# A prologue in an order of its own, and three of eight weight pairs rounded inside the main loop

## The chip, the cores and the metric

The kernel runs on one core of a Trainium2 chip. The metric is the device time of one execution in microseconds (us). Each median is over the executions named beside it. One execution of each kernel was recorded by the profiler; start times and durations below come from those records.

The core has a matrix engine (TensorE, PE in the profile, with PEld for its weight loads), VectorE (DVE), ScalarE (ACT), GpSimd (POOL), and a sync engine (SP) that here only issues transfers. Transfers are issued from SP, ACT and POOL; the profile counts them all on the same 16 DMA engines (in the first 180 us of the kernel before, 34.9% of these engines' time for SP's queue, 17.4% for ACT's and 12.6% for POOL's).

## The reference

```python
X = np.fft.rfft(x, axis=1)              # x: 8 batches x 3008 tokens x 256 channels
Y = X * (filt_r + 1j * filt_i)          # filters: 1505 frequencies x 256
y = np.fft.irfft(Y, n=3008, axis=1)
h = y.reshape(24064, 256) @ w_in        # 256 -> 2048
out = (h / (1 + np.exp(-h))) @ w_out    # silu(h) @ w_out, 2048 -> 256
```

The weights arrive as 64-bit floats and the kernel rounds them to 32 bits itself.

## The kernel before

The Fourier transform of a batch is a chain of small matrix products. **Stage 1** reads `x` in eight pieces (`load_x`), forms sums and differences on VectorE (`sums`), multiplies (`pa`), evicts from PSUM (`t`) and stores to DRAM (`d1`). **Six groups** then load that back (`t2`), run forward matmuls (`pb`), multiply by the filters on VectorE (`z`, `p`), add, run inverse matmuls (`pc`), evict (`q`) and store to DRAM (`d2`). **Stage 3** loads `t4`, multiplies (`pd`) and evicts to `y`. The main loop has 384 steps, bound by TensorE (busy for 49.86 of the first seven steps' 50.42 us), over all batches; the transforms of batch n+1 are spread over the steps of batch n. Only the first batch's transforms, and the rounding of the weights, lie ahead of the loop. The parts that matter, as they were:

```python
def load_filters():                       # 16 loads of 16 partitions each
    for j in range(4):
        s0, tau = slot_residue(0, 0, j), (1 if j % 2 == 0 else -1)
        for half in range(2):
            off, t = (s0, tau) if half == 0 else (94 - s0, -tau)
            for k, filt in enumerate((filt_r, filt_i)):
                p0 = 32 * j + 16 * half
                nc.scalar.dma_start(
                    out=f_t[k][p0:p0 + 16].rearrange("p g k c -> p (g k) c"),
                    in_=bass.AP(tensor=filt.tensor, offset=filt.offset + off * C,
                                ap=[[94 * C, 16], [t * C, 2 * NG], [1, C]]))

def evac(dst, src):                       # evictions alternate between two engines
    flip[0] ^= 1
    if flip[0]: nc.vector.tensor_copy(out=dst, in_=src)
    else:       nc.scalar.copy(out=dst, in_=src)

def add(g, k):                            # after the multiplication by the filters
    z, pt = prods[g][k]
    nc.vector.tensor_tensor(out=z[:, 0], in0=z[:, 0], in1=pt[:, 1], op=ALU.subtract)
    nc.vector.tensor_tensor(out=z[:, 1], in0=z[:, 1], in1=pt[:, 0], op=ALU.add)
# ... cut: stage 1, forward, multiply, inverse, stage 3, the main loop ...
def round_weights(j):                     # one of 16 weight matrices, 64 to 32 bits
    # ... cut: six instructions on VectorE, one on ScalarE, then on GpSimd:
    for w in range(2):
        gp.tensor_tensor(out=dst, in0=columns(mf[:, cols], w), in1=columns(ef[:, cols], w), op=ALU.mult)
    if j % 2:
        combine_weights(j // 2)           # four more on GpSimd for each pair
```

## Time and profile before

| | before |
|---|---|
| time, median of 3 (range) | 2809.41 us (2808.25 to 2809.86) |
| first forward matmul (`pb`) after stage 1 | 77.4 us |
| eviction of the last inverse (`q`, group 5) | 147.2 us |
| step 0 of the loop (its first copy `abc<-px`) | 180.25 us |
| steps 0 to 6, together | 50.42 us |
| first d1 store issued | 11.89 us |

The loop is TensorE's and is not touched after step 6, so the whole study is about the first 180 us, seven steps, and the last stores. The prediction shows the lines that say so.

### The profile page before, as it was taken

To read this page: it belongs to the slowest core of one execution; us is meant where nothing else is said; L and a number is where in the kernel's file an instruction comes from. 1 tells how busy PE (TensorE), PEld (TensorE's weight loads), DVE (VectorE), ACT (ScalarE), POOL (GpSimd) and SP (SyncE) were. 2 spreads that over 40 slices of the span, in tenths; PEclk is the share of its full clock that TensorE was granted. 3 is DMA by queue.
4 is the path that set the end of the run, shared out by engine and by line. 5 is a ranking of instruction groups with operands and counts; after the bars stand their busy time and mean duration, and the time that the engine had idled before them with its cause. 6 is when DMAs were issued, how large, how long until landed. Compare 5 with 4: busy or idle time off the path is not lost.

```text
span 2806.0 us, 39589 instructions
## 1 busy us (share of the span) xinstructions
PE 2671.0 (95%) x14592; PEld 2255.6 (80%) x14592; DVE 1671.9 (60%) x3528; ACT 1089.1 (39%) x2978; POOL 504.5 (18%) x739
## 2 busy tenths in 40 slices
PE   2469999999999999999999999999999999999997
PEld 0257889788897888878888888978888788898987
DVE  2866665666556665566655666566655666555554
ACT  0124334443344334443344433444344433444443
POOL 1531221112102120111111112012211211010100
PEclk9769999999999999999999999999999999999999
DMA  8543211232113211142103321133111422110000
GB/s 178 158 119 84 67 34 40 74 78 51 42 31 95 68 39 45 43 108 60 41 21 81 83 54 36 42 80 76 46 45 27 106 60 48 32 26 20 9 15 15
DMA packets 184546, 166.56 MB, mean 59 GB/s; under 512 B 121120, under 2 KB 151456, under 8 KB 184096
## 3 DMA queue, kind: packets, MB, share of 16 engines
q1 hardware_dynamic: 164624, 108.15, 16.0%
q0 software_dynamic: 17408, 50.35, 7.1%
q10 hardware_dynamic: 2320, 5.54, 1.1%
q8 instruction: 114, 1.87, 0.3%
q14 instruction: 80, 0.66, 0.1%
HBM read 88.97 MB, written 74.97 MB: 58 GB/s over the span
## 4 chain that ended last, share of the span: by engine, by line
PE 92%; DVE 4%; DMA 2%; issue 1%; POOL 0%; ACT 0%; SPq 0%; DVEq 0%; ACTq 0%; POOLq 0%
PE acc L467 40%; PE px L411 24%; PE pyz L411 17%; PE pd L341 4%; PE pc L319 3%; PE pa L267 2%; PE pb L290 2%; DVE g L382 1%; DMA x<-in_x_dram 1%; DVE u L255 1%; DVE z L310 0%; DMA d<-t 0%; DVE z L309 0%; DMA t<-d 0%; DMA filt<-in_filt_i_dram 0%
## 5 line engine op out<-in xcount | busy, mean ns | idle before, releaser
L467 PE MATMUL acc<-g,w_t 128*128 128x256 f32 (+1 forms) x5376 | 1512.6, 375 | 0.4 <-DVE g L382 0.4
L467 PEld LDWEIGHTS acc<-g,w_t 128*128 128x128 f32 x5376 | 1022.5, 190 | 114.4 <-DVE g L382 0.8
L382 DVE TENSOR_TENSOR g<-pyz,abc 128x256 f32<-128x256 f32 (+1 forms) x1152 | 479.7, 416 | 614.8 <-ACT abc L432 356.8
L382 DVE TENSOR_TENSOR g<-g 128x256 f32<-128x256 f32 (+3 forms) x1152 | 611.0, 530 | 196.6 <-ACT g L415 183.5
L411 PE MATMUL px<-ty,w_t 128*128 128x256 f32 (+1 forms) x2304 | 694.3, 383 | 0.5 <-ACT abc L432 0.5
L415 ACT ACTIVATE g<-g 128x256 f32<-128x256 f32 (+1 forms) x1152 | 473.0, 411 | 238.4 <-DVE g L382 235.9
L411 PEld LDWEIGHTS px<-ty,w_t 128*128 128x128 f32 x2304 | 419.5, 190 | 126.3 <-issue 72.1
L411 PE MATMUL pyz<-y,w_t 128*128 128x256 f32 (+1 forms) x1536 | 454.0, 377 | 8.5 <-DVE g L382 8.5
L382 POOL TENSOR_TENSOR s<-s 128x256 f32<-128x256 f32 (+1 forms) x329 | 265.7, 825 | 1040.4 <-DVE s L485 520.1
L411 PEld LDWEIGHTS pyz<-y,w_t 128*128 128x128 f32 x1536 | 282.9, 189 | 53.0 <-DVE g L382 15.8
L426 ACT COPY abc<-px 128x256 f32<-128x256 f32 (+1 forms) x384 | 141.4, 368 | 381.0 <-PE px L411 381.0
L415 ACT ACTIVATE g<-px 128x256 f32<-128x256 f32 (+1 forms) x384 | 145.8, 380 | 300.7 <-PE px L411 300.7
L432 ACT COPY abc<-px 128x256 f32<-128x256 f32 (+1 forms) x384 | 142.7, 372 | 285.0 <-PE px L411 284.8
L326 POOL DMA_DIRECT2D d<-q x192 | 113.9, 600 | 736.4 <-DVE q L209 736.3
L411 PE MATMUL pyz<-ty,w_t 128*128 128x256 f32 (+1 forms) x768 | 226.4, 377 | 0.0
L411 PE MATMUL px<-y,w_t 128*128 128x256 f32 (+1 forms) x768 | 225.7, 376 | 0.0
L411 PEld LDWEIGHTS pyz<-ty,w_t 128*128 128x128 f32 x768 | 145.7, 190 | 18.1 <-DVE g L382 2.0
L411 PEld LDWEIGHTS px<-y,w_t 128*128 128x128 f32 x768 | 144.7, 190 | 18.1 <-issue 0.4
L341 PEld LDWEIGHTS pd<-wi_t,t 96*128 96x128 f32 x1024 | 130.6, 201 | 21.4 <-issue 11.8
L341 PE MATMUL pd<-wi_t,t 96*128 96x94 f32 x1024 | 129.8, 283 | 17.6 <-issue 11.1
L319 PE MATMUL pc<-z,e_t 64*128 64x256 f32 x768 | 108.7, 422 | 37.3 <-DVE z L309 36.2
L419 ACT COPY abc<-px 128x256 f32<-128x256 f32 (+1 forms) x384 | 134.1, 349 | 0.1
(43 smaller groups left out, 1262.6 us busy)
## 6 DMA issues: line engine op xcount, KB each, us to landing
d<-t POOLq DMA_DIRECT2D x128, 192.0 KB, 3.0
t<-d SPq DMA_DIRECT2D x96, 256.0 KB, 4.1
d<-q POOLq DMA_DIRECT2D x192, 128.0 KB, 2.7
t<-d SPq DMA_DIRECT2D x64, 384.0 KB, 4.3
out_dram<-o SPq DMA_DIRECT2D x640, 32.0 KB, 1.8
x<-in_x_dram SPq DMA_DIRECT2D x128, 128.0 KB, 3.0
x<-in_x_dram SPq DMA_DIRECT2D x128, 60.0 KB, 2.9
raw<-in_moe_w_in_dram SPq DMA_DIRECT2D x16, 256.0 KB, 3.2
```

Source lines behind the costliest of these rows:

```text
L267: nc.tensor.matmul(out=ps[h][64 * par:64 * par + 64], lhsT=wf_t[rows, par], rhs=ut[rows, par], start=True, stop=True)
L290: nc.tensor.matmul(out=ps[k][32 * j:32 * j + 32, ri, :], lhsT=d_t[rows, 4 * g + at, ri, :], rhs=t2[rows, at, :], start=True, stop=True)
L319: nc.tensor.matmul(out=ps[i][:, k, :], lhsT=e_t[rows, g, k, ri, :], rhs=zs[k][rows, ri, :], start=(ri == 0), stop=(ri == 1))
L326: nc.gpsimd.dma_start(out=d2[a0:a0 + 2, :, :].rearrange("s n c -> n s c"), in_=qt[64 * p:64 * p + 64, :, :])
L341: nc.tensor.matmul(out=psv[:, i, :], lhsT=t4s[g][:, i, cb * 128:cb * 128 + 128], rhs=wi_t, start=True, stop=True)
L382: eng.tensor_tensor(out=out, in0=in0, in1=in1, op=op)
L411: nc.tensor.matmul(out=out, lhsT=w_t[:, c, 0, jp], rhs=rhs, start=start, stop=True, skip_group_check=True)
L415: nc.scalar.activation(out=g[:, k, 0:n], in_=g[:, k, 0:n] if src is None else src, func=AFT.Silu)
L419: nc.scalar.copy(out=sums[:, 0, 0:n], in_=xo)
L426: nc.scalar.copy(out=sums[:, 1, 0:n], in_=xo)
L432: nc.scalar.copy(out=sums[:, 2, 0:n], in_=xo)
L467: nc.tensor.matmul(out=acc[pair][i][:, h, 0:n], lhsT=w_t[:, c, 1, jp], rhs=g[:, k, 0:n], start=(jp == 0 and h == 0), stop=last, skip_group ...
```

## The change

Its intent: emit the first batch's transforms in a hand-made order instead of by the loop's plan. The loads come in the order of their use; `x` goes on two queues (sync and ScalarE); the filters move from ScalarE's queue to sync; the first batch's d2 stores move from GpSimd's queue to ScalarE's, and its adds from VectorE to GpSimd. One step of the rounding goes to ScalarE. Ten matrices are rounded ahead of the loop and six in steps 0 to 5. The last output stores use two queues.

```diff
 def load_filters():
-                    nc.scalar.dma_start(
+                    nc.sync.dma_start(
 def load_x(u):
+            if b == 0:
+                queue = (nc.sync, nc.scalar)[u % 2]
 def add(g, k):
-            nc.vector.tensor_tensor(...)        # both
+            eng = nc.vector if b > 0 else nc.gpsimd
+            eng.tensor_tensor(...)
 def inverse(g):
-                    nc.gpsimd.dma_start(out=d2[...], in_=qt[...])
+                    queue = nc.gpsimd if b > 0 else nc.scalar
+                    queue.dma_start(out=d2[...], in_=qt[...])
 def output(pair, chunk):
+                queue = nc.scalar if pair == len(pairs) - 1 and q % 2 else nc.sync
 def round_weights(j):
-        v.tensor_scalar(out=e, in0=e, scalar1=896.0, scalar2=0.0, op0=ALU.subtract, op1=ALU.max)
+        nc.scalar.activation(out=ef, in_=e, func=AFT.Relu, bias=bias_t)
# ... cut: buffers of their own for x, sums, raw and work ...
+    for u in range(8):
+        part["load_x"](u)
+    nc.sync.dma_start(out=d_t, in_=d_dram.ap())
+    weights(0)
+    load_filters()
# ... cut: sums and stage1 of the eight pieces, t2 loads, e table, weights 1 and 2, rounded 0 and 1 ...
+    for g in range(NG):
+        part["forward"](g)
+        for k in range(2):
+            part["multiply"](g, k)
+        for k in range(2):
+            part["add"](g, k)
+        if g > 0:
+            part["inverse"](g - 1)
+        if g % 2 == 0:
+            weights(3 + g // 2)
+        rounded(2 + g)
+    part["inverse"](NG - 1)
# ... cut: t4, rounded 8 and 9, stage 3 ...
+    for k in range(6):
+        put(k, 1, rounded, 10 + k)               # into steps 0 to 5
```

More of the change, by code (lines that the diff above doesn't have):

```diff
@@ L189 @@
     warm = cpool.tile([128, 1], FP32)
+    bias_t = cpool.tile([128, 1], FP32)
     x_t = [xpool.tile([128, 2, 2, C], FP32, name=f"x{i}") for i in range(2)]
@@ L234, in load_x @@
         def load_x(u):
-            if b == 0 and u < 4:
-                if u % 2 == 0:
-                    xs[u, "y"] = ypool.tile([128, 2, HALF], FP32, name=f"x_{b}_{u}", tag="y")
-                xs[u] = xs[u - u % 2, "y"][:, u % 2, 0:1024].rearrange("p (a n) -> p a n", a=2)
-                nc.gpsimd.memset(xs[u][32:64], 0.0)
+            queue = nc.sync
+            if b == 0:
+                queue = (nc.sync, nc.scalar)[u % 2]
+                if u in (0, 2):
+                    xs["y"] = ypool.tile([128, 2, HALF], FP32, name=f"x_{b}_{u}", tag="y")
+                if u < 4:
+                    xs[u] = xs["y"][:, u % 2, 0:1024].rearrange("p (a n) -> p a n", a=2)
+                elif u < 6:
+                    xs[u] = t4pool.tile([128, 2, 2 * C], FP32, name=f"x_{b}_{u}", tag="t4")
+                else:
+                    xs[u] = x_t[u % 2]
+                (nc.vector, nc.gpsimd)[u % 2].memset(xs[u][32:64], 0.0)
             else:
@@ L244, in load_x @@
                 for r0, nr in ((0, 32), (32, N1 - 32)):
-                    nc.sync.dma_start(
+                    queue.dma_start(
                         out=xs[u][64 * h + r0:64 * h + r0 + nr],
@@ L251, in sums @@
         def sums(u):
-            ut = upool.tile([128, 2, 512], FP32, name=f"u_{b}_{u}", tag="u")
+            if b > 0 or u % 3 == 0:
+                ut = upool.tile([128, 2, 512], FP32, name=f"u_{b}_{u}", tag="u")
+            else:
+                if u == 1:
+                    us["s"] = spool.tile([128, 2, 2, 512], FP32, name="u_s", tag="s")
+                ut = us["s"][:, u % 3 - 1]
             xt = xs.pop(u)
@@ L308, in add @@
             z, pt = prods[g][k]
-            nc.vector.tensor_tensor(out=z[:, 0], in0=z[:, 0], in1=pt[:, 1], op=ALU.subtract)
-            nc.vector.tensor_tensor(out=z[:, 1], in0=z[:, 1], in1=pt[:, 0], op=ALU.add)
+            eng = nc.vector if b > 0 else nc.gpsimd
+            eng.tensor_tensor(out=z[:, 0], in0=z[:, 0], in1=pt[:, 1], op=ALU.subtract)
+            eng.tensor_tensor(out=z[:, 1], in0=z[:, 1], in1=pt[:, 0], op=ALU.add)
         def inverse(g):
@@ L325, in inverse @@
                     a0 = p * NS + 2 * g + 12 * i
-                    nc.gpsimd.dma_start(out=d2[a0:a0 + 2, :, :].rearrange("s n c -> n s c"),
-                                        in_=qt[64 * p:64 * p + 64, :, :])
+                    queue = nc.gpsimd if b > 0 else nc.scalar
+                    queue.dma_start(out=d2[a0:a0 + 2, :, :].rearrange("s n c -> n s c"),
+                                    in_=qt[64 * p:64 * p + 64, :, :])
         def load_t4(g):
@@ L346, in stage3, with put, plan @@
                  psv)
+        return dict(load_x=load_x, sums=sums, stage1=stage1, load_t2=load_t2, forward=forward,
+                    multiply=multiply, add=add, inverse=inverse, load_t4=load_t4, stage3=stage3)
+    pending = []
+    def put(step, rnd, piece, *args):
+        pending.append((step + rnd / ROUNDS, len(pending), lambda: piece(*args)))
+    def plan(b, part):
         at = STEPS * b
-        pieces = []
-        def put(step, rnd, piece, *args):
-            pieces.append((at + step + rnd / ROUNDS, len(pieces), lambda: piece(*args)))
+        put(at - 49, 0, part["load_x"], 0)
+        put(at - 49, 0, part["load_x"], 1)
@@ L354, in spectral @@
         for u in range(8):
-            put(u - 48, 5, sums, u)
-            put(u - 47, 3, stage1, u)
-        put(-39, 0, load_t2, 0)
-        put(-39, 0, load_t2, 1)
+            put(at + u - 48, 5, part["sums"], u)
+            put(at + u - 47, 3, part["stage1"], u)
+        put(at - 39, 0, part["load_t2"], 0)
+        put(at - 39, 0, part["load_t2"], 1)
         for g in range(NG):
-            put(3 * g - (37 if b > 0 or g == 0 else 39), 3, forward, g)
-            put(3 * g - 37, 5, multiply, g, 0)
-            put(3 * g - 36, 1, multiply, g, 1)
-            put(3 * g - 36, 5, add, g, 0)
-            put(3 * g - 35, 1, add, g, 1)
-            put(3 * g - 35, 3, inverse, g)
@@ L367, in spectral @@
-        put(-18, 5, load_t4, 0)
-        for g, (step, rnd) in enumerate(((-16, 3), (-12, 3), (-8, 3), (-4, 3), (9, 3), (12, 6), (15, 6), (18, 6))):
-            put(step, rnd, stage3, 2 * g)
-            put(step, rnd, stage3, 2 * g + 1)
-        if b > 0:
-            put(-49, 0, load_x, 0)
-            put(-49, 0, load_x, 1)
-        return pieces, load_x
+            put(at + 3 * g - 37, 3, part["forward"], g)
+            put(at + 3 * g - 37, 5, part["multiply"], g, 0)
+            put(at + 3 * g - 36, 1, part["multiply"], g, 1)
@@ new lines, in plan, with plan_rest @@
+            put(at + 3 * g - 36, 5, part["add"], g, 0)
+            put(at + 3 * g - 35, 1, part["add"], g, 1)
+            put(at + 3 * g - 35, 3, part["inverse"], g)
+        put(at - 18, 5, part["load_t4"], 0)
+        for g, step in enumerate((-16, -12, -8, -4)):
+            for cb in range(2):
+                put(at + step, 3, part["stage3"], 2 * g + cb)
+        plan_rest(b, part)
+    def plan_rest(b, part):
+        for g, (step, rnd) in enumerate(((9, 3), (12, 6), (15, 6), (18, 6))):
+            for cb in range(2):
+                put(STEPS * b + step, rnd, part["stage3"], 8 + 2 * g + cb)
@@ L503, in output @@
                 p0 = 32 * q + 16 * rr
-                nc.sync.dma_start(
+                queue = nc.scalar if pair == len(pairs) - 1 and q % 2 else nc.sync
+                queue.dma_start(
                     out=bass.AP(tensor=out.tensor, offset=out.offset + t0 * C + 64 * q,
@@ L526, in columns, with load_weights @@
         return ap.rearrange("p (q k i) -> p k q i", q=4, k=2)
-    def load_weights(j):
-        raw = gpool.tile([128, 4, 512], U32, name=f"raw_{j}", tag="g")
-        nc.sync.dma_start(
-            out=raw[:, 0].rearrange("p (a n) -> p a n", a=2),
-            in_=moe_w_in.bitcast(U32)[:, 256 * j:256 * j + 256].rearrange("(a p) n -> p a n", p=128))
-        nc.sync.dma_start(out=raw[:, 1], in_=moe_w_out.bitcast(U32)[128 * j:128 * j + 128, :])
-        raws[j] = raw
+    def load_weights(jp):
+        if jp in (2, 5, 6, 7):
+            raw = spool.tile([128, 2, 2, 512], U32, name=f"raw_{jp}", tag="s")
+        else:
+            raw = gpool.tile([128, 2, 2, 512], U32, name=f"raw_{jp}", tag="g")
+        for i in range(2):
+            j = 2 * jp + i
+            nc.sync.dma_start(
+                out=raw[:, i, 0].rearrange("p (a n) -> p a n", a=2),
+                in_=moe_w_in.bitcast(U32)[:, 256 * j:256 * j + 256].rearrange("(a p) n -> p a n", p=128))
+            nc.sync.dma_start(out=raw[:, i, 1], in_=moe_w_out.bitcast(U32)[128 * j:128 * j + 128, :])
+        raws[jp] = raw
     def round_weights(j):
-        raw = raws.pop(j)
-        words = raw[:, 0:2].rearrange("p w (n t) -> p (w n) t", t=2)
+        words = raws[j // 2][:, j % 2].rearrange("p w (n t) -> p (w n) t", t=2)
         lo, hi = words[:, :, 0], words[:, :, 1]
-        e, m = raw[:, 2], raw[:, 3]
+        work = typool.tile([128, 2, 512], U32, name=f"work_{j}", tag="ty")
+        e, m = work[:, 0], work[:, 1]
         ef, mf = e.bitcast(FP32), m.bitcast(FP32)
@@ L547, in round_weights @@
                         op0=ALU.logical_shift_right, op1=ALU.bitwise_and)
-        v.tensor_scalar(out=e, in0=e, scalar1=896.0, scalar2=0.0, op0=ALU.subtract, op1=ALU.max)
-        v.tensor_scalar(out=e, in0=e, scalar1=255.0, scalar2=float(1 << 23),
+        nc.scalar.activation(out=ef, in_=e, func=AFT.Relu, bias=bias_t)
+        v.scalar_tensor_tensor(out=mf, in0=lo, scalar=2.0 ** -52, in1=mf, op0=ALU.mult, op1=ALU.add)
+        v.tensor_scalar(out=e, in0=ef, scalar1=255.0, scalar2=float(1 << 23),
                         op0=ALU.min, op1=ALU.mult)
@@ L552, in round_weights @@
                                op0=ALU.bitwise_and, op1=ALU.bitwise_or)
-        v.scalar_tensor_tensor(out=mf, in0=lo, scalar=2.0 ** -52, in1=mf, op0=ALU.mult, op1=ALU.add)
         for w in range(2):
@@ L559, in round_weights @@
         if j % 2:
+            raws.pop(j // 2)
             combine_weights(j // 2)
-        if j + 2 < NJ:
-            load_weights(j + 2)
     def load_exact(j):
@@ L579, in combine_weights @@
         combine(gp, w(S4), w(A12), w(S2), ALU.subtract)
-    def constants():
-        nc.scalar.dma_start(out=d_t, in_=d_dram.ap())
-        load_filters()
-        nc.scalar.dma_start(out=e_t, in_=e_dram.ap())
-        nc.scalar.dma_start(out=wi_t, in_=wi_dram.ap())
-    nc.sync.dma_start(out=wf_t, in_=wf_dram.ap())
-    for xt in x_t:
-        nc.gpsimd.memset(xt[32:64], 0.0)
-    pending = []
-    for b in range(B):
-        pieces, load_x = spectral(b)
-        pending += pieces
-        if b == 0:
-            for u in range(6):
-                load_x(u)
-            pending += [(-42.5 + k, 0, lambda k=k, load_x=load_x: load_x(6 + k)) for k in range(2)]
-            pending.append((-45, 0, constants))
@@ L600, with weights, rounded @@
-    if wide:
-        pending += [(-41.5, j, lambda j=j: load_weights(j)) for j in range(2)]
-        pending += [(-39 + 1.9 * j, NJ, lambda j=j: round_weights(j)) for j in range(NJ)]
-    else:
-        pending += [(-39 + 1.9 * j, NJ, lambda j=j: load_exact(j)) for j in range(NJ)]
+    def weights(jp):
+        if wide:
+            load_weights(jp)
+    def rounded(j):
+        if wide:
+            round_weights(j)
+        else:
+            load_exact(j)
+    nc.sync.dma_start(out=wf_t, in_=wf_dram.ap())
@@ new lines @@
+    nc.gpsimd.memset(bias_t, -896.0)
+    part = spectral(0)
+    for u in range(8):
[3 more added lines that the diff above has]
+    load_filters()
+    for u in range(3):
+        part["sums"](u)
+    for u in range(8):
+        part["stage1"](u)
+        if u + 3 < 8:
+            part["sums"](u + 3)
+    part["load_t2"](0)
+    part["load_t2"](1)
+    nc.sync.dma_start(out=e_t, in_=e_dram.ap())
+    weights(1)
+    weights(2)
+    nc.sync.dma_start(out=wi_t, in_=wi_dram.ap())
@@ new lines @@
+    rounded(0)
+    rounded(1)
+    for g in range(NG):
[10 more added lines that the diff above has]
+    part["inverse"](NG - 1)
+    part["load_t4"](0)
+    rounded(8)
+    rounded(9)
+    for u in range(8):
+        part["stage3"](u)
+    early[0] = None
@@ L605 @@
+    plan_rest(0, part)
+    for b in range(1, B):
+        plan(b, spectral(b))
+    for k in range(6):
+        put(k, 1, rounded, 10 + k)
+        if k in (1, 3):
+            put(k, 1, weights, 6 + k // 2)
     per = len(PAIRS) * 2
@@ L622 @@
     until(-1e-3)
-    early[0] = None
     for step in range(n_steps + LAG):
```

## The prediction

> **What bounds the kernel now.** I read three views: the page's slices, to see where TensorE is not busy; busy time by stage, to see what limits each part of that stretch; then waits and timeline inside it. The slices come first (PE busy tenths, 70 us a slice):
>
> ```profile
> PE   2469999999999999999999999999999999999997
> ```
>
> From the fourth slice on TensorE is full, so the time there is matmul time, which the change leaves alone. The first weight matmul of the main loop (L411) starts at 179.1 us; before it lie the first batch's transforms and the rounding of all weights. I cut these 179.1 us where the first forward matmul after stage 1 starts (77.4) and where the last inverse matmul ends (147.2). Columns: stretch, length, then busy time of PE, PEld, DVE, ACT, POOL, then clock, share of the 16 DMA engines, GB/s.
>
> ```profile
> 0.00:77.40 77.40, 21.52 (x66) 4.86 (x67) 21.95 (x37) 7.33 (x12) 17.45 (x31) 1.00 0.81 178
> 77.40:147.20 69.80, 32.29 (x286) 17.29 (x286) 60.42 (x108) 8.60 (x14) 41.16 (x58) 0.70 0.54 147
> 147.20:179.10 31.90, 14.34 (x65) 13.91 (x65) 23.41 (x35) 5.93 (x9) 20.90 (x26) 0.50 0.51 149
> ```
>
> Stage A is bound by transfers (engines of the DMA 81% busy, no compute engine over 28%); stage B by VectorE (60.4 of 69.8 us); stage C by a latency chain: store, load, matmul at half clock. The waits from 20 to 60 us say what A waits for (total us, times, longest):
>
> ```profile
> DVE t L209 <- DMA d<-t: 31.8, 2, 27.3
> ACT t L211 <- DMA filt<-in_filt_i_dram: 27.1, 1, 27.1
> ```
>
> The filter loads stand ahead of ScalarE's evictions in its own instruction stream and ahead of the d1 stores in the transfer engines. For B, the timeline shows what VectorE pays beside GpSimd (start, us, engine, line; the adds L309 and L310 are 128x256, 0.42 us when GpSimd is quiet):
>
> ```profile
> 93.71 0.65 DVE L309 TENSOR_TENSOR z<-z,p 128x256 f32<-128x256 f32 x1
> 94.16 3.39 POOL L382 TENSOR_TENSOR w_t<-w_t 128x256 f32<-128x256 f32 x4
> 94.29 0.94 DVE L310 TENSOR_TENSOR z<-z,p 128x256 f32<-128x256 f32 x1
> ```
>
> [...] the same add takes 0.42 us alone and 0.94 beside GpSimd. [...] the share was 0.95 from 20 to 40 us with three queues in use. [...] 0.73 us (2.90 for four) when undisturbed and 0.84 on average, against 0.42.
>
> **The change, part by part.** Stage A. The order by engine shows x going on two queues, then on the sync queue the d table, the first weight pair, the filters, the t2 loads, and only then the e table. Transfer work before the first forward matmul: over the first 180 us the sync queue took 34.9% of 16 engines for 16.99 MB (62.8 us, 3.7 us per MB), the GpSimd queue 12.6% for 6.29 MB (3.6 us per MB), the ACT queue 17.4% for 5.54 MB (31.3 us). The two tables are 2.36 MB of the last, 8.7 us at 3.7, so the filters (3.15 MB, runs of 1 KB in half of them) cost 22.6 us. Then x 3.08 MB = 11.4; d1 stores 3.15 MB = 11.3; d table 0.79 MB = 2.9; first weight pair 1.05 MB = 3.9; filters 22.6; first t2 half a MB = 1.9. Sum 54 us, plus 2 us until the first transfer and some 5 us of gaps (a tenth; a guess from the shares of 0.95 at best): 61 us for what starts at 77.4 now. Gone from in front of it are the e table (5.8 us) and the idle 19% . Gain 16.
>
> Stage B. VectorE loses 24 adds, and rounding falls from 16 matrices of six VectorE instructions to ten of five, eight of them before the last inverse is evicted. Per group g it then has four multiplies (0.60 us pitch, 2.4), one eviction (0.6) and one rounding. The rounding's own pitch is 0.33+0.46+0.61+0.46+0.61 = 2.5 us, but two of its instructions now wait for two ScalarE activations (0.63 each), and the order on ScalarE puts two d2 stores, an eviction (0.58) and two more stores ahead of these: 4 x 0.45 (the issue time of a filter load there) + 0.58 + 2 x 0.63 = 3.6 us after VectorE's eviction, and then 1.1 us for the last two instructions: 4.8 us for the rounding. So a group takes 2.4 + 0.6 + 4.8 = 7.8 us. GpSimd needs per group four adds, two products and on average two combinations, 8 x 0.85 = 6.8 us: just under, and off the path. The first two groups are slower by some 6 us in all, since e table and two weight pairs (3.7 MB, about 14 us) come only after t2: group 1's multiplies stand behind a rounding that waits for the second pair. From the first forward to the last inverse's eviction: 2 + 5 x 7.8 + 6 + the last group's 2.4 + 0.6 + 3.0 (its rounding is not delayed by much) = 53 us, against 69.9 (77.4 to 147.3). Gain 17.
>
> Stage C. Now the t4 loads stand behind weight loads that wait for roundings; the first is issued at 154.0, the third at 166.75. Afterwards two t4 loads go out as soon as the stores land: eviction and stores 5.5 us, load 4.3, then four groups of two at 3.6 us (7.11 us for four, half clock as now) plus about a microsecond for the third load: 25 us against 31.8. Gain 7. In sum the loop starts at 61 + 53 + 25 = 139 us, 40 earlier.
>
> What is moved into the loop. Six roundings fall into steps 0 to 5. A step there now looks so:
>
> ```profile
> 200.90:208.20 7.30, 7.30 (x38) 5.47 (x37) 4.57 (x10) 3.00 (x8) 1.00 (x2) 1.00 0.39 107
> ```
>
> VectorE has 4.57 us of work in 7.30; a rounding adds 2.6 us, GpSimd gets 1.5 us of products and every second step 3 us of combinations[...]. It fits by sum, but not by order: ScalarE's two activations stand ahead of the px copy that TensorE's next accumulation needs, and about 2 us late that copy eats most of the 1.1 us that the stage-1 matmuls give. I take 1 us a step, 6 us in all (an estimate, 2 to 12).
>
> The end. The last sixteen stores are issued one after another:
>
> ```profile
> 2796.01 7.51 SPq L504 DMA_DIRECT2D out_dram<-o  x16
> ```
>
> On two queues the issue takes half: 3.5 us off.
>
> Sum: 2809.4 - 40 + 6 - 3.5 = 2772 us.
>
> **The rivals.** First, stage 1 stays starved: the sync queue may have up to eight transfers outstanding, which in the filter phase are 1.5 MB or 11 us of slow traffic, and the d1 stores, two tiles deep, wait behind them as now (12 us from issue to landing at 44 us). For it: exactly this wait is in the trace. Against: the sum of transfers is the same in whatever order they are served, and once the filters are in, the last d1 stores find the engines free. It would make A 68 to 72: total 2780 to 2785. Second, GpSimd becomes the bound of B: it is at 6.8 us of a group's 7.8[...]; with roundings in between its instructions measured up to 0.98 us each (3.91 for four), then a group takes 9 us: 6 us more, 2778. Third, the ScalarE round trip is hidden because the sequencer issues stores faster than 0.45 us, and the groups run at VectorE's 5.5 us: 12 us less, 2760. Fourth, the loop's first steps hide the roundings wholly: 2766. Fifth, TensorE's clock, granted at half from 147 us on, comes back later than now: against it, it was full again 16 us after the loop's start, at 195 us, and the loop's start is unchanged.
>
> **Range and chances.** The three stage gains are uncertain by about 8, 8 and 4 us, the steps by 5; taken as independent some 13 us in all, so 2752 to 2792 should hold it 8 times in 10 (a little wider than 1.3 x 13, for what I have not seen). Faster by over 2% means under 2753.2: the prologue would have to shrink by some 59 us of 179, to 120, which needs the first and third doubts to fall well together: 0.12. Slower by over 2% needs a stall in the loop that goes on after step 5; nothing there is changed: 0.01.
>
> **What would show it.** In the changed profile: first forward matmul near 61 us, with the filter wait gone from ScalarE; q evictions about 7.8 us apart, each rounding's third VectorE instruction waiting on ScalarE; first L411-type matmul near 139; steps 0 to 5 about 8.3 us each and 7.26 after; a final store issue of about 4 us. If the forward matmul starts before 52 or after 70, the transfer sum is wrong; if groups are not paced by ScalarE, the chain in B is; if steps 0 to 5 take over 9.5 us each, the cost in the loop is.

Measured in the kernel before: the 128x256 add on VectorE, the share of the DMA engines, and an instruction of that size with two inputs on GpSimd (2.90 us for four of them from 76.98 us on; 0.838 us each over all 32 combinations of the weights), which the "8 x 0.85" of stage B rests on. The first rival's "up to eight transfers outstanding" can be read in the trace of the changed kernel: the fourth filter load (23.98 us) is issued only when the d table, eight places ahead of it on the sync queue, has landed, the next four when the four weight loads have, and the last eight when the first eight filter loads have.

## More of the kernel before

One line is added here, for what comes later: the seven first steps of the kernel before in one stretch (stretch, length, then busy time and instructions of PE, PEld, DVE, ACT and POOL, then clock, DMA share, GB/s).

```profile
180.25:230.67 50.42, 49.86 (x233) 36.20 (x234) 32.35 (x65) 20.43 (x56) 6.11 (x12) 0.96 0.37 98
```

TensorE is busy for 49.86 of 50.42 us and VectorE for 32.35: the steps have room on VectorE.

## The result

| | before | after | predicted after |
|---|---|---|---|
| time, median of 4 (range) | 2808.83 (2806.55 to 2809.86) | 2780.32 (2779.0 to 2781.49) | 2772 (2752 to 2792) |
| first forward matmul | 77.4 | 65.2 | 61 |
| first multiply, group 0 | 79.45 | 68.31 | – |
| eviction of the last inverse | 147.2 | 122.2 | 114 |
| step 0 of the loop | 180.25 | 147.62 | 140 |
| steps 0 to 6, together | 50.42 | 58.28 | 56.4 |
| from step 7 to the end | 2575.3 | 2571.9 | 3.5 less |

The changed kernel takes 0.9899 of the time before (95% interval 0.9882 to 0.9917): 28.5 us less, which is within 2%. Ratios here are the mean time of one kernel's runs over that of the other's of the same rounds, so not quite the ratio of the medians. The three parts add up: 32.6 us from the start, minus 7.9 in the steps, plus 3.4 at the end make 28.1; the profiled spans differ by 28.2.

In the page of the changed kernel TensorE's row of slices (tenths busy, 40 slices) differs from before only at its ends:

```profile
PE   3599999999999999999999999999999999999998
```

The same three stages as in the prediction, with the same columns, cut at the changed kernel's own events:

```profile
0.00:65.20 65.20, 18.51 (x65) 4.80 (x66) 24.65 (x39) 8.67 (x14) 15.72 (x30) 1.00 0.91 182
65.20:122.20 57.00, 33.50 (x288) 18.00 (x288) 36.82 (x59) 10.39 (x17) 32.91 (x46) 0.88 0.76 213
122.20:146.50 24.30, 14.08 (x65) 13.90 (x65) 10.35 (x16) 5.54 (x8) 10.43 (x14) 0.52 0.43 109
```

Stage A is 12.2 us shorter, stage B 12.8, stage C 7.6. A is more clearly a stage of transfers than before (share 0.91, was 0.81), yet it moves data at much the same rate (182 GB/s, was 178). In B, VectorE has lost its full row: 36.82 us of 57.00, where it was 60.42 of 69.80. Something else paces B now.

What waits in stage A (us in total, times, longest):

```profile
ACT t L211 <- DMA d<-t: 35.6, 6, 12.8
DVE t L209 <- DMA d<-t: 31.9, 5, 11.4
...
ACT t L211 <- DMA x<-in_x_dram: 14.5, 1, 14.5
```

Evictions of stage 1 wait for earlier d1 stores to land (the eviction's buffer is one of two), as before; and one new wait of 14.5 us ahead of ScalarE's very first eviction. The experiment that puts `x` back on one queue shows what it is worth.

In stage B, one group on ScalarE (start, us, engine, line, operation, tiles; ACTq is ScalarE's sequencer issuing transfers):

```profile
98.61 1.24 ACTq L340 DMA_DIRECT2D d<-q  x2
99.97 0.58 ACT L211 COPY q<-pc 128x512 f32<-128x512 f32 x1 [5.57 <-DVE work L574]
100.58 1.24 ACTq L340 DMA_DIRECT2D d<-q  x2
101.93 0.63 ACT L575 ACTIVATE work<-work 128x512 f32<-128x512 uint32 x1 [1.37 <-issue]
```

and what VectorE does about it:

```profile
102.59 0.69 DVE L579 SCALAR_TENSOR_TENSOR work<-raw,work 128x512 f32<-128x512 uint32 x1 [2.30 <-ACT work L575]
```

Two stores, the eviction, two more stores, and only then the activation that the rounding on VectorE waits 2.30 us for: the chain that the prediction had named. A store takes 0.62 us to issue. The groups' first multiplies start at 68.31, 77.39, 86.16, 95.50, 104.27 and 113.46 us: 9.03 us apart, not 7.8. The first of these intervals (9.08) has another cause than the four after it (8.77 to 9.34): group 0 has no stores ahead of its rounding, and VectorE waits for the weights instead:

```profile
74.58 0.43 DVE L574 TENSOR_SCALAR work<-raw 128x512 uint32<-128x512 uint32 x1 [3.79 <-DMA raw<-in_moe_w_out_dram]
```

The seven first steps, to be held against the line of before shown above:

```profile
147.62:205.90 58.28, 51.66 (x233) 35.26 (x234) 51.75 (x95) 26.70 (x68) 27.17 (x36) 0.98 0.45 121
```

VectorE goes from 32.35 to 51.75 us busy, GpSimd from 6.11 to 27.17, and TensorE idles for 6.6 us. Steps 1 to 5 take 8.61 to 8.63 each, step 6 again 7.28.

The last stores, on two queues side by side:

```profile
2771.31 3.70 SPq L529 DMA_DIRECT2D out_dram<-o  x8
2771.32 3.92 ACTq L529 DMA_DIRECT2D out_dram<-o  x8
```

### The profile page after: what moved, and what is told of

The parts are those of the page before. It is cut to its first block, busy times and chain, and to the rows that moved or that the text cites. A ratio compares the mean times of both kernels' runs of the same rounds, so it can differ in the third digit from the quotient of the medians.

```text
span 2777.8 us, 39564 instructions
## 1 busy us (share of the span) xinstructions
PE 2670.7 (96%) x14592; PEld 2253.3 (81%) x14592; DVE 1657.2 (60%) x3492; ACT 1098.0 (40%) x2994; POOL 505.1 (18%) x738
## 4 chain that ended last, share of the span: by engine, by line
PE 91%; DVE 4%; DMA 3%; ACT 1%; issue 1%; POOL 0%; ACTq 0%; SPq 0%; DVEq 0%; POOLq 0%
PE acc L491 39%; PE px L435 24%; PE pyz L435 17%; PE pd L355 4%; PE pc L332 3%; PE pa L279 2%; PE pb L302 2%; DMA d<-t 1%; DVE g L406 1%; DVE u L267 1%; DMA t<-d 1%; DMA x<-in_x_dram 0%; DVE z L323 0%; DMA raw<-in_moe_w_out_dram 0%; DVE z L322 0%
## 5 line engine op out<-in xcount | busy, mean ns | idle before, releaser
L340 POOL DMA_DIRECT2D d<-q x168 | 99.3, 597 | 728.1 <-DVE q L209 720.3
L284 POOL DMA_DIRECT2D d<-t x128 | 65.5, 516 | 329.7 <-ACT abc L456 283.7
```

The lines of the kernel that those rows point to most:

```text
L284: nc.gpsimd.dma_start(out=d1[par].rearrange("s p n c -> (s p) n c")[:, 4 * u:4 * u + 4, :], in_=t1[64 * par:64 * par + 2 * NS].rearrange(" ...
L340: queue.dma_start(out=d2[a0:a0 + 2, :, :].rearrange("s n c -> n s c"), in_=qt[64 * p:64 * p + 64, :, :])
```

## The experiments

Twelve kernels ran, in three calls of four, each on another chip; each has its own runs of the kernel before, whose medians were 2809.79 (7 runs), 2808.48 (7) and 2809.18 (7). Each experiment has four timed runs, its median and range below. "The changed kernel" is 2780.32 throughout. One warning from the profiles: with stage A untouched, the first multiply of group 0 still fell anywhere from 61.7 to 69 us between executions. So a start time from a single profile is worth several us.

### Stage B: what paces the groups

**The rounding ahead of the previous group's inverse** (so that its activations stand ahead of the stores on ScalarE).

```diff
             part["add"](g, k)
+        rounded(2 + g)
         if g > 0:
             part["inverse"](g - 1)
         if g % 2 == 0:
             weights(3 + g // 2)
-        rounded(2 + g)
```

> Edit: in the group loop each rounding stands before the inverse of the previous group, so that ScalarE has its two activations before the four d2 stores (4 x 0.62 us) and the eviction. Theory S (groups of stage B are paced by ScalarE: the rounding's third VectorE instruction waits for an activation behind four store issues): the rounding takes about 3 us in place of 5.5, the group period falls from 9.0 to about 6.8 to 7.2 (then GpSimd, eight instructions), stage B some 10 us shorter, about 2770 us. Rival G (GpSimd's eight instructions[...] pace the groups): no change within 2 us, 2779 to 2781.

Measured: 2776.21 us (2775.51 to 2778.8), ratio 0.9883 [0.9868, 0.9897]; groups 7.9 us apart on average ((108.42 - 68.99) / 5), and about 7.2 from group 1 on. The order on ScalarE did pace them. But the gain is 4 us, not five times 1.8: only four intervals have stores ahead of the rounding. Group 0 waits for its weights in both kernels (5.15 us in this profile, 3.79 in the other) and lasts 10.4 us, and from the last group's first multiply to the last eviction it is 10.5 us where it was 8.8.

**The first batch's d2 stores on the sync queue.**

```diff
-                    queue = nc.gpsimd if b > 0 else nc.scalar
+                    queue = nc.gpsimd if b > 0 else nc.sync
```

> Edit: the first batch's d2 stores are issued by the sync queue in place of ScalarE. Theory S: 2.5 us of issue a group leave ScalarE, so the period falls from 9.0 to about 7 and the kernel is about 10 us faster, unless the sync queue's own order (stores wait for evictions ahead of t2 and weight loads) delays a load; then 5. Rival G: no change within 2 us.

Measured: 2773.83 us (2771.63 to 2776.04), ratio 0.9873 [0.9856, 0.9889]; groups 8.0 us apart, the last eviction at 115.44, the loop from 140.11. ScalarE in one group:

```profile
89.97 0.59 ACT L211 COPY q<-pc 128x512 f32<-128x512 f32 x1 [7.03 <-DMA d<-q]
90.46 0.63 ACT L575 ACTIVATE work<-work 128x512 f32<-128x512 uint32 x1
```

The activation follows the eviction at once, so the issue of stores was the cost. In its place there is a new wait: the eviction's own buffer is one of two and waits for a store to land (`DMA d<-q`).

**The adds back on VectorE.**

```diff
-            eng = nc.vector if b > 0 else nc.gpsimd
+            eng = nc.vector
```

> Edit: the first batch's complex adds back on VectorE. Theory S: VectorE gets four adds of 0.34 us pitch before the eviction that everything on ScalarE waits for, so each of six groups is about 1.4 us longer: 8 us slower, 2788. Rival G: GpSimd loses four of its eight instructions a group (3 us), the period falls to 7 or less: about 10 us faster, 2770.

Measured: 2790.6 us (2784.22 to 2791.28), ratio 0.9927 [0.9912, 0.9942]: 10 us worse, with groups 10.6 us apart. The stage of the groups in this kernel's profile:

```profile
61.20:121.00 59.80, 31.13 (x263) 18.08 (x254) 41.45 (x80) 8.97 (x15) 14.84 (x20) 0.79 0.66 185
```

GpSimd falls to 14.84 us of 59.80 and the groups get slower, so GpSimd does not bound them (the second rival of the prediction). This edit also gives VectorE more to do; but the rounding-first kernel leaves GpSimd's work as it was, and its groups came down to 7.2 us. Moving the adds was worth some 10 us. The profile is of the fastest of the four runs, with an early stage A (first multiply at 61.67), which is why its loop start, 149.89, looks less bad than the median.

**Both: rounding first, and stores on sync.** The edits are the first two together.

> Edit: d2 stores of the first batch on the sync queue and rounding before the inverse, together. Theory S: once ScalarE is out of the way the groups run at GpSimd's 6.8 us or VectorE's 6.0[...], some 7 us each, so little is won over the stores on sync alone (whose groups took 8.0): about 3 us, 2771. Rival: both waits were independent and the two gains (4 and 6.5 us) add up: 2769 to 2770.

Measured: 2775.57 us (2774.59 to 2777.72), ratio 0.9881 [0.9867, 0.9896]. The two gains do not add; it is no better than the stores alone. The last eviction came at 117.83, against 115.44.

**Both, but the last group in the changed kernel's order** (rounding first only for `g < NG - 1`).

```diff
+        if g < NG - 1:
+            rounded(2 + g)
         if g > 0:
             part["inverse"](g - 1)
         if g % 2 == 0:
             weights(3 + g // 2)
-        rounded(2 + g)
+        if g == NG - 1:
+            rounded(2 + g)
```

> Stores of the first batch's d2 on the sync queue, and the rounding ahead of the inverse for all groups but the last, where the order stays as changed. If the last group's rounding ahead of its inverse is what made the two together no better than the stores alone: last inverse's eviction 2 to 3 us sooner than with both (117.8), loop start at 138 to 140, time 2769 to 2772. If instead the group's period is by then set by VectorE, whatever the order: groups of 7.5 us as with the stores alone, time 2773 to 2776.

Measured: 2773.76 us (2772.93 to 2776.44), ratio 0.9874 [0.9859, 0.9889]: equal to the stores alone, so the first theory's 2769 to 2772 failed and the rival's range holds, though not its reason. Groups are 7.9 us apart and the last eviction falls at 116.38. VectorE's evictions of the last two groups show what stands there:

```profile
109.69 0.69 DVE L209 COPY q<-pc 128x512 f32<-128x512 f32 x1 [1.23 <-DMA d<-q]
...
116.38 0.69 DVE L209 COPY q<-pc 128x512 f32<-128x512 f32 x1 [2.46 <-DMA d<-q]
```

VectorE is not full; its evictions wait for earlier stores to land before they may reuse their buffer. This is in the trace of this kernel; a kernel with a third buffer was not tried.

### Stage A: what fills the first 65 us

**The reversed filter rows read forwards.** Half of the filter loads read rows backwards, so that each row of 1 KB is a run of its own; here all read forwards in runs of 12 KB. The result is WRONG on purpose.

```diff
                 off, t = (s0, tau) if half == 0 else (94 - s0, -tau)
+                if t < 0:
+                    off, t = off - 2 * NG + 1, 1
                 for k, filt in enumerate((filt_r, filt_i)):
```

> Wrong result on purpose: the four loads of each filter that run backwards (runs of 1 KB) read the same rows forwards (runs of 12 KB). Same bytes. Theory T (stage A is the sum of the transfers, of which the filters are by far the dearest per byte): the first multiply starts some 5 us earlier than the 66 to 69 us of most runs so far, and the kernel is about 5 us faster, 2775. Rival Q (stage A is the queueing of d1 stores behind whatever is outstanding; the filters' slowness is their 16 partitions, not their direction): within 2 us of 2780.

Measured: 2781.72 us (2781.3 to 2783.44), ratio 0.9902 [0.9885, 0.9918]. Nothing changes: the first 66 us move 178 GB/s at a share of 0.90, where the first 65.2 us of the changed kernel move 182 at 0.91. The prediction's reason for slow filters, runs of 1 KB, falls.

**The filters after the first two t2 loads.**

```diff
     weights(0)
-    load_filters()
     ...
     part["load_t2"](1)
+    load_filters()
```

> Edit: the filter loads are issued after the first two t2 loads, so that the d1 stores have only the d table and the first weight pair beside them. Theory T: stage 1 ends much earlier (its evictions no longer wait 12 us for a store), but the filters' 23 us then stand between t2 and the first multiply: the multiply starts where it did, 66 to 69 us, or up to 4 us later, as the engines idle a little during stage 1 and the e table and weights come as much later; 2780 to 2785. Rival Q: the waits were lost time, and the first multiply starts 5 us earlier: 2775.

Measured: 2784.85 us (2782.85 to 2785.89), ratio 0.9913 [0.9898, 0.9927]: 4.5 us worse, first multiply at 73.62. Stage 1 is no longer starved (first forward matmul at 44.65), and VectorE's first multiply waits for filters:

```profile
73.62 0.69 DVE L314 TENSOR_TENSOR z<-pb,filt 128x512 f32<-128x512 f32 x1 [29.86 <-DMA filt<-in_filt_r_dram]
```

Whoever is served first, the filters' time has to be paid. This order also shows that time nearly by itself: the first filter load is issued at 43.82 and the multiply starts at 73.62, 29.8 us later, with no stage-1 store left beside them. But t2 loads still land until 48.5 us, and from 64.2 us on the e table and weights are under way too. A stretch in the middle, in which the filters are nearly all that is being moved, counts 133 GB/s at a share of 1.07, at which 3.15 MB take some 24 us (an estimate). The prediction had 22.6 us for it.

```profile
46.00:64.00 18.00, 3.99 (x62) 1.49 (x56) 0.00 (x0) 0.00 (x0) 2.14 (x4) 1.00 1.07 133
```

**The same bytes of filters in loads of 128 partitions.** Two loads in place of sixteen, one in runs of 12 KB and one in runs of 1 KB. Its output is wrong, which doesn't matter for the time.

```diff
-        for j in range(4): ...                  # 16 loads, each to f_t[k][p0:p0 + 16]
+        for k, filt in enumerate((filt_r, filt_i)):
+            nc.sync.dma_start(
+                out=f_t[k].rearrange("p g k c -> p (g k) c"),
+                in_=bass.AP(tensor=filt.tensor, offset=filt.offset,
+                            ap=[[10 * C, 128], [(1 + k) * C, 2 * NG], [1, C]]))
```

> WRONG on purpose: the same 3.15 MB of filters come in 2 loads of 128 partitions each (half of it in runs of 12 KB, half in runs of 1 KB, as in the changed kernel) in place of 16 loads of 16 partitions each; their values are not the right ones, the times don't depend on that. Theory D (the filters are slow because each load goes to 16 partitions [...]): the queue gets through them in about 10 us instead of some 21, the first multiply starts at 56 to 61 us instead of 66 to 70, and the time falls by 7 to 11 us, to about 2770. Rival V (what costs is the volume of all loads, 5.9 MB with weights and x, whatever partitions they go to): first multiply unchanged at 66 to 70, time 2778 to 2783.

Measured: 2764.71 us (2762.17 to 2765.18), ratio 0.9838 [0.9824, 0.9853]: 15.6 us better than the changed kernel, more than the 7 to 11 expected. First multiply at 51.95, loop from 131.31. The stretch in which the filters move, first in the changed kernel, then in this one (the last two numbers are DMA share and GB/s):

```profile
21.00:45.00 24.00, 6.85 (x27) 1.80 (x24) 5.58 (x9) 1.75 (x3) 3.01 (x6) 1.00 1.06 215
```

```profile
21.00:33.00 12.00, 4.51 (x19) 1.19 (x16) 3.69 (x6) 1.17 (x2) 2.01 (x4) 1.00 1.02 393
```

The DMA engines look equally full in both (1.06 and 1.02), and move 215 GB/s in one and 393 in the other. A full share is no proof of a full rate. The edit was made for the number of partitions that a load reaches, 16 before and 128 here, and the runs agree with theory D in direction: 133 GB/s where the filters moved nearly alone, in loads of 16 partitions, is about a third of 393. Why loads to few partitions should be slow was not shown. This run changes the number of loads, from 16 to 2, and the order of rows in DRAM as well, so the share of each is not separated.

**x on one queue again.**

```diff
-                queue = (nc.sync, nc.scalar)[u % 2]
+                queue = nc.sync
```

> All x loads of the first batch on the sync queue again (the loads by use, the adds and all else as changed). Theory T (stage A is bound by the sum of all transfers, and the two queues only change who issues): first multiply at 66 to 71 us, time within 3 us of the changed kernel, 2778 to 2783. Rival Q (two queues bring x sooner, or give it a larger share beside the filters): first multiply 4 us or more later, time 2784 or more. Rival R (the issues of x on ScalarE hold up its first evictions, which now wait until 16.8 us): the first stores go 3 us or more sooner and the first multiply comes 2 to 5 us sooner.

Measured: 2773.02 us (2772.15 to 2773.88), ratio 0.987 [0.9855, 0.9885]: 7.3 us better than the changed kernel, with no overlap between the four runs of each. Undoing this part of the change helps. ScalarE's beginning in the changed kernel, then with x on one queue:

```profile
2.47 14.25 ACTq L252 DMA_DIRECT2D x<-in_x_dram  x14
16.76 1.07 ACT L211 COPY t<-pa 128x512 f32<-128x512 f32 x2 [14.52 <-DMA x<-in_x_dram]
```

```profile
8.95 0.58 ACT L211 COPY t<-pa 128x512 f32<-128x512 f32 x1 [6.71 <-PE pa L279]
11.07 0.58 ACT L211 COPY t<-pa 128x512 f32<-128x512 f32 x1 [1.54 <-PE pa L279]
```

Fourteen issues hold ScalarE for 14.25 us, a microsecond each, so its first eviction, whose input had long been ready, runs at 16.76 us instead of 8.95. The second queue saved hardly any issue time in return: the 32 issues of x end at 16.7 us on two queues and at 17.6 on one, where the sync engine needs half a microsecond for each. GpSimd's first d1 stores follow from it, in the changed kernel and with one queue:

```profile
17.64 2.18 POOL L284 DMA_DIRECT2D d<-t  x4 [13.15 <-DVE u_s L267]
```

```profile
12.31 1.19 POOL L284 DMA_DIRECT2D d<-t  x2 [7.81 <-DVE t L209]
14.43 1.01 POOL L284 DMA_DIRECT2D d<-t  x2 [0.93 <-DVE t L209]
```

With one queue, three of eight pieces are on their way when the first filter load is issued (20.44 us) and the fourth follows at 21.00; with two queues there are two (the filters begin at 21.11), and the last ones go out at 56.63 instead of 44.47. First forward matmul: 56.8 against 65.2. The kernel before issued its first d1 store at 11.89, so this start was lost by the change itself. Rival R of the expectation named it and sized it at 2 to 5 us; the theory that two queues are neutral missed.

### The loop: what the six roundings cost

**The Relu back on VectorE** (one activation less on ScalarE, one instruction more on VectorE).

```diff
-        nc.scalar.activation(out=ef, in_=e, func=AFT.Relu, bias=bias_t)
+        v.tensor_scalar(out=e, in0=e, scalar1=896.0, scalar2=0.0, op0=ALU.subtract, op1=ALU.max)
```

> Edit: the second activation of the rounding (Relu with bias) is again a VectorE instruction, as before the change. In stage B, theory S: the second activation runs beside VectorE's third instruction, so nothing is won there and VectorE gets 0.46 us a rounding that lies in its wait for the first activation: period unchanged within 0.3 us, stage B within 2 us. In steps 0 to 5, theory P (the px copies are late because they stand behind two activations): the copy comes 0.55 us earlier, the step shrinks from 8.61 to about 8.2, 2 to 3 us faster in all. Rival V (the steps are long because VectorE has too much to do): VectorE gets 0.46 us more a step, steps 0.3 to 0.5 us longer, 2 to 3 us slower in all.

Measured: 2781.07 us (2779.32 to 2782.53), ratio 0.9898 [0.9883, 0.9913]; steps 2 to 5 unchanged at 8.61 to 8.63 (step 1 takes 8.78), groups 9.2 us apart. TensorE's waits around the first steps, in the changed kernel (146 to 200 us):

```profile
PE px L435 <- ACT abc L450: 3.3, 6, 0.8
PE pyz L435 <- DVE g L406: 2.6, 5, 0.7
```

and with the Relu on VectorE (140 to 200 us):

```profile
PE pyz L435 <- DVE g L406: 4.8, 6, 1.0
...
PE px L435 <- ACT abc L450: 0.5, 2, 0.3
```

The wait for the px copy on ScalarE, the mechanism in the prediction, nearly goes away and the step is as long as before: here it was the wait that happened to end last, not what set the length. The wait for VectorE takes its place. The edit is a swap, though: an instruction on VectorE in place of a wait there for ScalarE. In step 3 of both kernels VectorE needs the same 2.80 us from the first instruction of the rounding to its eviction of stage 1. So this run alone doesn't say what a lighter ScalarE would be worth.

**No GpSimd work of the rounding in the loop** (neither products nor combinations for matrices 10 to 15; a fill ahead of the loop in place of their results). Its output is wrong, which doesn't matter for the time.

```diff
-        for w in range(2):
+        for w in range(2 if j < 10 else 0):
...
-            combine_weights(j // 2)
+            if j < 10:
+                combine_weights(j // 2)
...
+    nc.gpsimd.memset(w_t[:, :, :, 5:8], 0.0)
```

> Wrong result on purpose: in steps 0 to 5 GpSimd's products and combinations of the rounded weights are left out (their places in w_t are set to zero at the start); VectorE's and ScalarE's part of the rounding stays. Theory L (VectorE's row sets these steps, and [...] stretches the two sums from 1.28 to 1.7 to 2.4 us and the two g subtractions): steps 0 to 5 shrink from 8.61 to about 7.6, 6 us faster in all, 2774. Rival W (VectorE's own instructions fill the step, without GpSimd): within 0.2 us of 8.61, 2780.

Measured: 2777.48 us (2776.95 to 2778.17), ratio 0.9887 [0.9873, 0.9902]. Its seven steps, and one pair of VectorE's sums for the next batch, first in the changed kernel and then here:

```profile
178.34 2.36 DVE L267 TENSOR_TENSOR u<-x 111x512 f32<-111x512 f32 x2
```

```profile
149.23:203.70 54.47, 51.35 (x233) 37.07 (x234) 45.72 (x95) 26.75 (x68) 6.08 (x12) 0.93 0.47 130
...
194.42 1.28 DVE L267 TENSOR_TENSOR u<-x 111x512 f32<-111x512 f32 x2
```

The steps' excess over the kernel before (50.42) falls from 7.9 to 4.1 us. VectorE runs the same 95 instructions in 45.72 us instead of 51.75: the 6 us are instructions stretched beside GpSimd, as with the two sums, 2.36 us against 1.28.

The 4.1 us hold two other things. Step 0 took 8.41 us here and 7.91 in the changed kernel, but at a clock of 0.54 here and 0.82 there. In step 2, 8.42 us long, VectorE waited 0.76 us for weights to land, and TensorE then 1.1 us for the px copy behind ScalarE's two activations: when that copy comes later still, it does hold TensorE. Steps 1, 3, 4 and 5 took 7.56 to 7.61 us; step 3 of the changed kernel, then of this one:

```profile
172.75:181.38 8.63, 7.56 (x37) 5.34 (x36) 7.73 (x14) 4.02 (x11) 3.65 (x5) 1.00 0.52 163
```

```profile
173.62:181.22 7.60, 7.27 (x38) 5.39 (x37) 6.70 (x14) 4.02 (x11) 1.01 (x2) 1.00 0.49 147
```

A step before the change took 7.26 us. So GpSimd's work getting in VectorE's way is 1.0 of the 1.35 us by which such a step grew, as the expectation had it for a step; the other third of a microsecond is not explained.

**The second batch's stage-1 evictions all on ScalarE**, on top of the kernel with the last group's order kept.

```diff
-                evac(t1[:, h], ps[h])
+                if b == 1:
+                    nc.scalar.copy(out=t1[:, h], in_=ps[h])
+                else:
+                    evac(t1[:, h], ps[h])
```

> As the run before (label best), and both evictions of the second batch's first stage on ScalarE in steps 1 to 8, instead of one of two. Theory V (steps 0 to 5 are as long as VectorE's row of work, which is full at 8.61 us): 0.6 us less on VectorE in each of five to six steps, these at 7.9 to 8.1 us, time 2.5 to 3.5 us under the run before. Rival P (the sequence of products waits for ScalarE): steps 8.6 or longer, up to 9, time the same or 1 to 2 us more.

Measured: 2776.75 us (2773.53 to 2778.01), ratio 0.9881 [0.9864, 0.9897]: some 3 us worse than without this edit by the medians, though the ranges overlap. The seven steps and one moment on ScalarE in them:

```profile
143.29:202.35 59.06, 54.16 (x233) 35.85 (x234) 47.62 (x89) 29.09 (x73) 26.71 (x36) 0.93 0.44 121
...
173.03 1.06 ACT L283 COPY t<-pa 128x512 f32<-128x512 f32 x2
173.97 0.39 ACT L459 COPY abc<-px 128x256 f32<-128x256 f32 x1
```

VectorE has 4 us less to do (47.62, was 51.75) and steps 1 to 5 are no shorter: 8.60 to 8.66. (Of the 0.8 us between 59.06 and 58.28, 0.5 is step 0, again at a clock of 0.54.) In the step shown, VectorE waits 0.66 us for the copy at 173.97, which stands behind the two evictions that were moved there: a wait has taken the place of the eviction, and the row of VectorE is as long as before. So VectorE's busy total does not set the step; the three kernels fit its instructions in order with their waits for ScalarE, a row that became shorter only where GpSimd's work was gone. How to get under 8.6 us with that work present was not found.

## Why the prediction was right or wrong

The time was 8.3 us over the predicted 2772 and well inside the range. By its own steps, in the profiled executions: the loop starts 32.6 us earlier and not 40, the steps cost 7.9 and not 6, and the end was right. That is 9.3 us; the medians differ a little from the profiled executions, and the kernel before was 0.6 us faster in these runs.

**What bounds the kernel, and where the gain lies: right.** Only the start, seven steps and the end moved, and stage by stage the gains had the right sign and order.

**Stage A, 61 us: measured 65.2.** The step that failed is "x going on two queues", which the prediction charged nothing. It held ScalarE until 16.7 us and cost the time 7.3 us. Without it the first forward matmul comes at 56.8 us, under the predicted 61, so the sum of transfers was too high by some 4 us, and the two errors partly cancelled, which is luck (in single profiles, which vary by several us here). The term of 22.6 us for the filters is near the 24 us estimated from their rate nearly alone, but its reason, runs of 1 KB, was wrong: with forward reads nothing changed, and with 128 partitions per load everything in that stretch went at 393 GB/s. On the other side, d1 stores and filters together moved at 215 GB/s, well over the filters' own rate (133), which suggests that such loads leave room beside them and that the terms of the sum do not simply add; no run tested that by itself. The trace of the changed kernel shows that a second issuing engine also pays issue time, 14.25 us for 14 issues, on an engine that had other work. The first rival (d1 stores starved, A at 68 to 72, total 2780 to 2785) had the wait right, and its total came true, though A ended at 65.2; but the kernel with the filters after the t2 loads shows that un-starving by itself wins nothing.

**Stage B, 53 us: measured 57.0.** The mechanism was right, shown by the two kernels that shortened ScalarE's queue ahead of the activation. The mis-sized term is the issue of a d2 store, four of them per group: 0.45 us taken from a filter load, 0.62 measured. (The kernel before issued the same stores from GpSimd at 0.62 us each, so the size was there to be read.) With short gaps between the instructions, the rounding takes 5.77 us from the end of VectorE's eviction (98.50 to 104.27) in place of 4.8, and groups 1 to 4 together 4.9 us more than four times 7.8. VectorE's stretched instructions (0.93 us beside GpSimd, 0.42 alone) add little: in the group shown, the two that precede the activation's result end at 100.29, and VectorE then waits. The last group took 8.8 us and not 6.0, because its rounding waited for ScalarE like the others (2.30 us), where the prediction had it hardly delayed; the start of the stage took 3.1 and not 2. Against these, group 0 with its wait for weights took 9.08 us, where 7.8 and 6 us were written. The second rival, a 9 us group bound by GpSimd, had the number and the wrong engine: with GpSimd at half the work the group was slower, and with all of its work but the rounding first, faster.

**Stage C, 25 us: measured 24.3.** Right.

**The loop, 6 us: measured 7.9.** The size was within the stated 2 to 12, the mechanism wrong: the px copy behind two activations is there, and as late as predicted (3.46 us into step 3, 1.4 before the change), but with that wait nearly gone the steps were as long. GpSimd's stretching of VectorE (two sums in step 3: 2.36 us beside it, 1.28 without it), which the prediction saw in the adds (0.94 us against 0.42) and then did not price, is 1.0 of the 1.35 us by which a step at full clock grew. The rest is left open. The fifth rival, a clock that comes back later, did not meet the profiled execution of the changed kernel but did meet others: with the stores on sync, step 0 ran at 0.50 where the changed kernel had 0.82, and steps 0 and 1 took 17.6 us, not 16.5. In the kernel before, the clock was full again from 186 us (1.00 from 186 to 190, 0.66 on average from 180 to 186), not 195 as the prediction read.

**The end, 3.5 us: measured 3.4.** Right.

Six kernels that differ from the changed one by a line or a few beat both kernels and are correct; the best three are x on one queue (2773.02), stores on sync (2773.83) and that with the rounding moved for all groups but the last (2773.76). One queue for x and stores on sync were not tried in one kernel. A correct kernel whose filters go to more partitions at a time was not written either; the run with wrong values says that up to 15.6 us lie there.

## What to carry to other kernels

An issue of a transfer takes time of the engine that makes it (14 issues of x held ScalarE for 14.25 us): before spreading loads or stores over a second queue, count what that engine has to do next and who waits for it, at the issue time that this shape shows in a trace. Here a d2 store took 0.62 us of ScalarE, a filter load 0.31 to 0.32 of the sync engine once each had to wait for an earlier one, and an x load about 1 us on each of two queues and 0.51 on one. A DMA share near 1 does not say that data moves at full rate (215 GB/s at 1.06, 393 at 1.02); compare GB/s between stretches, and try loads that reach more partitions (133 GB/s with 16 nearly alone; 393 in the stretch with 128, where the loads were also fewer). And a wait that ends last names a suspect, not the cause: twice here it was all but removed (stage 1's stores, the px copy) and the time did not fall.
